# Slot attention into two mixture layers: phi held stationary for the P products, buffers named one by one, a new list of issue

## The chip, the cores and the metric

The kernel runs on one core of a Trainium2 chip. The metric is the device time of one execution in microseconds (us), the median of three runs. A profile of one execution goes with it. A difference of 0.3% (1.4 us) is about what a measurement of this kernel can tell from no change.

## The reference

Eight samples of eight heads are computed, 576 positions and head dimension 64, all in fp32:

```python
a = softmax(phi, axis=2)                      # 8 x 8 x 576 x 32, over the 576 positions
k_m, v_m = a^T k, a^T v                       # 32 memory rows per head
attn = softmax(q k_m^T / 8)                   # 576 x 32 per head
x = concat_heads(attn v_m)                    # 4608 x 512
h = max(x w1, x w2, x w3)                     # 4608 x 768
y = h w_out                                   # 4608 x 512, input of the second layer
logits = y phi2                               # 4608 x 32, 8 experts of 4 slots
slot_in = softmax(logits, axis=0)^T y
slot_out[e] = relu(slot_in[e] w1e[e]) w2e[e]  # 8 experts, 512 -> 1024 -> 512
out = softmax(logits, axis=1) slot_out
```

## The kernel before, in words

The 4608 x 512 matrix x is never formed. For a sample n the kernel multiplies its eight v_m by the weights first (V1 = v_m w, `v1m`, L563) and then the attention by V1 (`mn`, L596). The 768 columns of h are worked in six chunks i of 128. A unit is a pair (n, i): 48 units. For each unit there are two halves hf of 288 positions and three weights r, so 288 products `mn`, each of six matmuls (the attention and V1 are split into a high and a low part, `ah`, `al`, `vh`, `vl`) into one of three PSUM banks `m`. `ev` empties the bank: ACT copies r = 0 to g1 (L606), DVE takes the maximum for r = 1 (L608) and for r = 2 into ht (L610).

Stages of a sample, in the order in which they depend on each other: load phi transposed (`phit`), its maximum (`mxr`, DVE L373), exponential (`pe`, ACT L389), transpose on PE (`ptm`, L396) and copy (`ptc`, L401); k_m and v_m (`km`, 40 matmuls for the two halves of the heads, L438), normalized (`kmr`, `kmc`), transposed (`kvtm`, `kvtc`); scores (`scm`, L474), transposed by DVE (`sct`, L480), softmax (`s1r`, `s1s`, `s1e`, `s2s`, `s2m`), transposed back (`s3t`, L517), split into `ah` (ACT `s3h`, L527) and `al` (POOL `s3l`, L531). `vh` and `vl` are the split of V1 (`v1h` ACT L572, `v1l` DVE L578). For n = 0 the whole chain has to run before the first product can.

The weights come as 64-bit words and are brought to fp32 on the chip, in 17 chunks x: load (`raw`), ReLU with a scale on ACT (`cva`, L310) into a scratch buffer cz, a scaling of the low word on ACT (`cvb`, L314), a shift on DVE (`cvd`, L319), an addition on POOL (`cvp`, L324, 1.3 us for 512 columns and 1.8 for 768).

P = w_out phi2 (768 x 32) gives the logits straight from h. Before, each of its six chunks is a transpose of w_out (`pt`, L333), a copy (`pc`) and four matmuls with the transposed weights stationary and phi2 moving (`pm`, L342), and a copy (`po`).

`warm n` is n matmuls of the identity with itself (L800) that nothing reads. A matmul of fp32 has two records in the trace (a transpose one). In the tail, the eight experts are computed from 64 pieces of weights of 512 KB (`send`, one DMA each on SP's queue, L287; a few in four parts, L285). 44 buffers hold pieces; the first pieces are sent during the main part, into space of finished stages. The pieces of `more2` (L287, 383 us) need the space that the last `mn` and `ev` give up. Then come the remaining sends, as the experts give buffers up, and 18 output DMAs of 512 KB (L1091).

What sets the order of the work is a list written out by hand, `ORDER`: each word calls one of the functions above, every engine and SP's queue work in the order of this list, and semaphores do the rest. PSUM banks and the buffers g1, ht, vh and vl come from pools; which buffer a request gets is left to the pool.

Of the kernel before, what the change touches and what calls it, by code (L numbers as in the profile page):

```python
# [8 lines left out]
FR = mybir.dt.float32r  # L9
# [13 lines left out]
for _x in (2, 3, 4, 5, 12, 6, 7, 13, 8, 9, 14, 15, 10, 11):  # L23
# [135 lines left out]
)  # L159
W = [1, 0, 0, 3, 2]  # L160
NH = 4
LL = 0
# [1008 lines left out]
```

## Time and profile before

| | us |
|---|---|
| median of three runs (453.47 to 454.70) | 454.24 |
| the profiled execution, its own time | 454.55 |
| its span, first to last instruction | 452.8 |
| mean granted TensorE clock | 0.986 |

The span lies 1.75 us below the time of its own execution. Times in the rows are from the start of the span. In a chain of waits a row is: start, duration, engine, tile, line, records. In a timeline a row ends with what released the engine. A row with L800 is a warm product.

### The profile page before, as it was taken

To read this page: it belongs to the slowest core of one execution; us is meant where nothing else is said; L and a number is where in the kernel's file an instruction comes from. 1 tells how busy PE (TensorE), PEld (TensorE's weight loads), DVE (VectorE), ACT (ScalarE), POOL (GpSimd) and SP (SyncE) were. 2 spreads that over 40 slices of the span, in tenths; PEclk is the share of its full clock that TensorE was granted. 3 is DMA by queue.
4 is the path that set the end of the run, shared out by engine and by line. 5 is a ranking of instruction groups with operands and counts; after the bars stand their busy time and mean duration, and the time that the engine had idled before them with its cause. 6 is when DMAs were issued, how large, how long until landed. Compare 5 with 4: busy or idle time off the path is not lost.

```text
span 452.8 us, 12542 instructions
## 1 busy us (share of the span) xinstructions
PE 431.8 (95%) x5233; PEld 361.1 (80%) x5233; DVE 317.5 (70%) x736; ACT 192.3 (42%) x450; POOL 70.2 (16%) x92
## 2 busy tenths in 40 slices
PE   6989999999999999999999999999999999999990
PEld 5778889879888879978888887988887899655580
DVE  1275687578877996698779978898956453578480
ACT  2576777645443343343323342443434132222370
POOL 0243645520020003002100020020110000011000
PEclk9999999999999999999999999999999999999985
DMA  8987994307402293627657766378473956999997
GB/s 309 415 329 271 330 417 139 145 13 288 175 4 112 92 350 121 240 71 243 195 199 239 264 251 231 120 249 302 134 276 100 387 186 204 376 403 409 406 369 308
DMA packets 42249, 109.49 MB, mean 242 GB/s; under 512 B 3408, under 2 KB 20048, under 8 KB 40144
## 3 DMA queue, kind: packets, MB, share of 16 engines
q1 hardware_dynamic: 42192, 108.69, 65.5%
q8 instruction: 41, 0.67, 0.6%
q14 instruction: 16, 0.13, 0.1%
HBM read 91.38 MB, written 17.30 MB: 240 GB/s over the span
## 4 chain that ended last, share of the span: by engine, by line
PE 90%; DVE 3%; DMA 3%; ACT 1%; issue 1%; ACTq 0%; DVEq 0%
PE m L596 52%; PE x L563 8%; PE l L800 5%; PE x L438 4%; PE x L747 2%; PE l L679 2%; DMA more<-in_e_w_dram 2%; PE x L474 2%; PE m L1018 2%; PE x L638 2%; PE x L342 1%; PE l L1035 1%; PE x L1079 1%; PE m L1079 1%; PE x L333 1%
## 5 line engine op out<-in xcount | busy, mean ns | idle before, releaser
L596 PE MATMUL m<-ah,vh 128*128 128x288 f32 x576 | 171.0, 312 | 0.6 <-DVE ht L610 0.6
L596 PE MATMUL m<-ah,vl 128*128 128x288 f32 x576 | 161.6, 295 | 0.0
L596 PEld LDWEIGHTS m<-ah,vh 128*128 128x128 f32 x576 | 108.2, 188 | 19.3 <-issue 13.2
L596 PE MATMUL m<-al,vh 128*128 128x288 f32 x576 | 123.3, 295 | 0.0
L596 PEld LDWEIGHTS m<-ah,vl 128*128 128x128 f32 x576 | 108.4, 188 | 0.3
L596 PEld LDWEIGHTS m<-al,vh 128*128 128x128 f32 x576 | 92.3, 188 | 0.3 <-POOL al L531 0.3
L606 ACT ACTIVATE g<-m 128x288 f32<-128x288 f32 x96 | 39.1, 411 | 71.2 <-PE m L596 62.9
L608 DVE TENSOR_TENSOR g<-m,g 128x288 f32<-128x288 f32 x96 | 42.7, 450 | 33.8 <-PE m L596 28.4
L572 ACT ACTIVATE vh<-x 128x384 fp32r<-128x384 f32 (+1 forms) x100 | 42.0, 477 | 54.7 <-PE x L563 40.7
L610 DVE TENSOR_TENSOR ht<-m,g 128x288 f32<-128x288 f32 x96 | 42.5, 451 | 22.1 <-PE m L596 11.6
L578 DVE TENSOR_TENSOR vl<-x,vh 128x384 fp32r<-128x384 f32 (+1 forms) x100 | 48.8, 531 | 7.3 <-ACT vh L572 7.1
L563 PE MATMUL x<-arena,kvt 64*32 64x384 f32 (+1 forms) x800 | 39.5, 477 | 1.2 <-DVE vl L578 0.8
L531 POOL TENSOR_TENSOR al<-arena,ah 128x576 fp32r<-128x576 f32 x16 | 22.8, 1433 | 74.3 <-ACT ah L527 54.6
L800 PE MATMUL l<-cst 128*128 128x128 f32 x162 | 25.5, 307 | 4.0 <-DMA cst<-in_consts_dram 3.4
L324 POOL TENSOR_TENSOR arena<-arena 128x768 uint32<-128x768 uint32 (+1 forms) x13 | 23.5, 1811 | 34.8 <-ACT arena L314 27.4
L800 PEld LDWEIGHTS l<-cst 128*128 128x128 f32 x162 | 22.0, 211 | 7.3 <-DMA cst<-in_consts_dram 3.4
L615 POOL COPY arena<-ht 128x64 f32<-128x64 f32 x24 | 6.3, 279 | 123.7 <-DVE ht L610 97.8
L563 PEld LDWEIGHTS x<-arena,kvt 64*32 64x32 f32 x800 | 12.2, 105 | 13.6 <-issue 8.2
L642 DVE STREAM_TRANSPOSE arena<-ht 128x512 f32<-128x512 f32 x30 | 20.5, 697 | 0.2
L438 PE MATMUL x<-arena 128*32 128x129 f32 x640 | 19.6, 274 | 0.5 <-ACT arena L401 0.5
L438 PEld LDWEIGHTS x<-arena 128*32 128x32 f32 x640 | 17.4, 110 | 2.2 <-ACT arena L401 0.7
L480 DVE STREAM_TRANSPOSE arena<-x 128x288 f32<-128x288 f32 x32 | 13.4, 458 | 5.2 <-PE x L474 5.1
(266 smaller groups left out, 571.4 us busy)
## 6 DMA issues: line engine op xcount, KB each, us to landing
arena<-in_e_w_dram SPq DMA_DIRECT2D x44, 512.0 KB, 7.9
arena<-in_w_dram SPq DMA_DIRECT2D x14, 768.0 KB, 5.1
arena<-in_kv_dram SPq DMA_DIRECT2D x8, 1290.0 KB, 9.5
arena<-in_q_dram SPq DMA_DIRECT2D x16, 576.0 KB, 6.1
arena<-in_kv_dram SPq DMA_DIRECT2D x8, 1032.0 KB, 6.4
tr<-arena SPq DMA_DIRECT2D x30, 256.0 KB, 2.8
hbuf<-tr SPq DMA_DIRECT2D x30, 256.0 KB, 3.8
out_dram<-arena SPq DMA_DIRECT2D x10, 512.0 KB, 5.7
```

What stands on the lines that cost most here:

```text
L324: (eng or nc.gpsimd).tensor_tensor(out=du, in0=du, in1=lo.bitcast(U32), op=ALU.add)
L438: nc.tensor.matmul(t[32 * g:32 * g + 32, 0:KVC], phin_sb[:, j, b, 32 * g:32 * g + 32], kv_sb[:, j, b, g] if j < 4 else kv4_sb[:, g], start ...
L531: nc.gpsimd.tensor_tensor(out=al[n][:, :, c], in0=aT_sb[:, :, c], in1=ah[n][:, :, c].bitcast(FP32), op=ALU.subtract)
L563: nc.tensor.matmul(t[b][32 * g:32 * g + 32, 128 * r0:128 * r1], kvt[n][r, b, 32 * g:32 * g + 32], w_sb[r, i, r0:r1, g], start=True, stop=T ...
L572: nc.scalar.activation(out=v1[n, i][0][:, b, c], in_=ph["v1", n, i][b][:, c], func=ACTF.Copy)
L578: nc.vector.tensor_tensor(out=vl[:, b, c], in0=ph["v1", n, i][b][:, c], in1=vh[:, b, c].bitcast(FP32), op=ALU.subtract)
L596: nc.tensor.matmul(t[:, 0:HALF], x, y, start=(k == 0), stop=(k == 5))
L606: nc.scalar.activation(out=g1[u, hf], in_=t[:, 0:HALF], func=ACTF.Copy)
L608: nc.vector.tensor_tensor(out=g1[u, hf], in0=t[:, 0:HALF], in1=g1[u, hf], op=ALU.max)
L610: nc.vector.tensor_tensor(out=ht[n, i][:, cs], in0=t[:, 0:HALF], in1=g1.pop((u, hf)), op=ALU.max)
L642: nc.vector.transpose(out=v, in_=ht[n, i][:, 0:512])
L800: nc.tensor.matmul(t[:, 0:128], ident, ident, start=True, stop=True)
```

## The change

1. `ORDER` is replaced: the same work otherwise, in a new order on every engine and on SP's queue. `warm` is called for 34 products ahead of the steady part, where there were 81.
2. Banks and the buffers g1, ht, vh, vl are named one by one: a table `SLOTS` says for each request which buffer it takes.
3. The ReLU of the weights writes its destination, and the shift works on it in place; the four scratch buffers cz go.
4. P: phi2 is stationary in four column groups and three transposed chunks move at once (`pq`), a copy (`pr`), and three matmuls with that as the stationary operand and `sel` moving (`pm`), which add the four groups. Twice, for six chunks.
5. The first V (n = 0, i = 0), computed in three pieces r, has two banks of its own for each piece; before, the three pieces shared two banks.

```diff
-    "cst; warm 3; warm 2; warm 4; warm 3; warm 3; warm 1; phit 0; mxr 0; pe 0 0; pe 0 1; raw 2; warm 4; ptm 0 2; "
-    "ptm 0 0; warm 1; ptc 0 0; warm 4; ptm 0 1; ptc 0 1; warm 1; kv 0 0; km 0 1 0 2; kv 0 1; cva 2; cvd 2; raw 0; "
-    "ptc 0 2; cvb 2; cvp 2; cva 0; km 0 0 0 2; km 0 0 2 5; kmr 0 0; kmc 0 0; km 0 1 2 5; kmr 0 1; kmc 0 1; warm "
-    "3; kvtm 0; cvd 0; q 0 0; q 0 1; warm 1; kvtc 0; scm 0 0; sct 0 0; cvb 0; cvp 0; s1r 0 0; raw 1; cva 1; cvb "
-    "1; scm 0 1; sct 0 1; warm 1; warm 11; s1s 0 0; s1e 0 0; cvd 1; raw 3; cva 3; s1r 0 1; warm 4; raw 4; cvb 4; "
-    "cva 4; s2s 0 0; cvd 3; s2m 0 0; warm 9; cvp 1; s1s 0 1; v1m 0 0 1 2; v1h 0 0 1 2; v1m 0 0 0 1; cvb 3; v1h 0 "
-    "0 0 1; v1l 0 0 1 2; s3t 0 0; cvp 3; s1e 0 1; kv 1 0; phit 1; v1m 0 0 2 3; s3h 0 0; v1h 0 0 2 3; warm 8; warm "
-    "11; s2s 0 1; raw 6; cva 6; cvb 6; s3l 0 0; mn 0 0 1; mxr 1; pe 1 0; raw 5; warm 7; pe 1 1; cvd 4; ptm 1 0; "
...
-    "mn 47 1 2; mn 47 0 2; ev 47 1 1; trm 7 2; trc 7 2; ltm 0 3; dtm 6; dtc 6; ev 47 0 2; trm 7 1; trc 6 3; trc 6 "
-    "2; trm 7 4; trc 7 1; ev 47 1 2; trm 7 3; ltc 0 3; lg 7 1; slm 6 0; trc 7 3; slm 6 1; lg 7 2; lg 7 3; trc 7 "
-    "4; sla 6 0; sla 6 1; lg 7 4; hrc 47"
+    "phit 0; cst; warm 3; mxr 0; kv 0 0; pe 0 0; ptm 0 0; kv 0 1; warm 3; pe 0 1; ptm 0 1; ptm 0 2; ptc 0 2; raw "
+    "2; ptc 0 1; warm 3; km 0 1 0 2; warm 2; km 0 1 2 5; raw 0; ptc 0 0; km 0 0 0 2; cva 2; kmr 0 1; kmc 0 1; km "
+    "0 0 2 5; kmr 0 0; cvb 2; cvd 2; warm 3; cvp 2; kmc 0 0; kvtm 0; cva 0; cvd 0; q 0 0; kvtc 0; scm 0 0; warm "
+    "4; cvb 0; cvp 0; raw 1; cva 1; sct 0 0; q 0 1; warm 2; scm 0 1; s1r 0 0; cvb 1; s1s 0 0; cvd 1; cvp 1; warm "
+    "5; v1m 0 0 1 2; warm 2; sct 0 1; s1e 0 0; s2s 0 0; s2m 0 0; raw 3; cva 3; cvd 3; cvb 3; cvp 3; phit 1; v1h 0 "
+    "0 1 2; v1m 0 0 0 1; v1h 0 0 0 1; s3t 0 0; raw 4; s1r 0 1; warm 1; raw 5; v1l 0 0 0 1; s3h 0 0; s3l 0 0; cvb "
+    "4; warm 6; v1m 0 0 2 3; v1h 0 0 2 3; v1l 0 0 1 2; mn 0 0 1; cva 4; cva 5; mxr 1; pe 1 1; pe 1 0; v1l 0 0 2 "
+    "3; mn 0 0 2; s1s 0 1; s1e 0 1; cvd 4; kv 1 0; mn 0 0 0; ptm 1 2; ptc 1 2; ptm 1 1; ptc 1 1; cvd 5; ptm 1 0; "
+    "ptc 1 0; kv 1 1; ev 0 0 0; cvp 4; v1m 0 1; v1h 0 1; s2s 0 1; s2m 0 1; s3t 0 1; v1l 0 1; s3h 0 1; s3l 0 1; ev "
+    "0 0 1; km 1 1; km 1 0; cvb 5; cvp 5; raw 6; kmr 1 0; cvb 6; mn 1 0 0; ev 1 0 0; cva 6; ev 0 0 2; raw 7; kmc "
...
+    "44 1 2; ev 44 1 2; trc 6 4; mn 46 1 0; mn 46 0 0; ev 46 0 0; mn 44 0 2; ev 44 0 2; trm 7 1; trc 7 1; trm 7 "
+    "0; trc 6 3; dtm 6; dtc 6; trc 7 0; mn 46 0 1; ev 46 0 1; hrc 44; mn 46 1 1; ev 46 1 0; ev 46 1 1; mn 47 1 2; "
+    "slm 6 0; lg 7 0; lg 7 1; mn 47 0 1; mn 47 0 0; ev 47 1 2; hrc 47; ev 47 0 0; mn 47 0 2; mn 46 1 2; ev 47 0 "
+    "1; ev 47 0 2; mn 46 0 2; hrc 42; ltm 0 3; ev 46 1 2; trm 7 2; send 1; send 1; send 1; send 1; send 1; send "
+    "1; send 1; sla 6 0; trm 7 3; trc 7 3; ev 46 0 2; trm 7 4; trc 7 4; send 1; send 1; lg 7 2; lg 7 3; slm 6 1; "
+    "lg 7 4; sla 6 1; trc 7 2; hrc 45; send 1; send 1; send 1; ltc 0 3; hrc 46"
...
+    def buf(pool, tag, shape, dtype, count):
+        if tag not in picks:
+            return pool.tile(shape, dtype, tag=tag, name=tag, bufs=count)
+        j = int(next(picks[tag]))
+        if (tag, j) not in fixed:
+            fixed[tag, j] = pool.tile(shape, dtype, tag=tag + "_%d" % j, name=tag + "_%d" % j, bufs=1)
+        return fixed[tag, j]
+
     def bank(pool, tag):
-        return pool.tile([128, 512], FP32, tag=tag, name=tag)
+        return buf(pool, tag, [128, 512], FP32, {"m": 3, "x": 4, "l": 1}[tag])
...
-        nc.scalar.activation(out=z, in_=hi, func=ACTF.Prelu, scale=2.0 ** -112, alpha=2.0 ** 32)
+        nc.scalar.activation(out=dst, in_=hi, func=ACTF.Prelu, scale=2.0 ** -112, alpha=2.0 ** 32)
...
-        nc.vector.tensor_scalar(out=du, in0=zu, scalar1=3, scalar2=None, op0=ALU.logical_shift_left)
+        nc.vector.tensor_scalar(out=du, in0=du, scalar1=3, scalar2=None, op0=ALU.logical_shift_left)
...
-        for k in range(4):
-            nc.tensor.matmul(
-                t[:, 0:32], wt_sb[i][:, 128 * k:128 * k + 128], phi2_sb[:, k], start=(k == 0), stop=(k == 3))
+    def p_q(y):
+        ph["pq", y] = t = mx()
+        o = wt_all[y].rearrange("p (j k c) -> p k j c", j=3, k=4)
         for k in range(4):
             nc.tensor.matmul(
+                t[32 * k:32 * k + 32, 0:384], phi2_sb[:, k], o[:, k], start=True, stop=True, tile_position=(0, 32 * k))
+    def p_r(y):
+        nc.scalar.activation(out=pq_sb[y], in_=ph["pq", y][:, 0:384], func=ACTF.Copy)
+    def p_m(y):
+        ph["pm", y] = t = mx()
+        for j in range(3):
+            nc.tensor.matmul(
+                t[:, 32 * j:32 * j + 32], pq_sb[y][:, 128 * j:128 * j + 128], sel[:, 0:M], start=True, stop=True)
...
-        if ("v1", n, i) not in ph:
-            ph["v1", n, i] = [mx() for _ in range(2)]
-        t = ph["v1", n, i]
+        ph["v1", n, i, r0] = t = [mx() for _ in range(2)]
```

Both lists send 31 pieces before the tail. In the old one sends 18 to 29 stand together after 253 of the 288 products `mn`, 30 and 31 after 264 and 273. In the new one send 18 stands after 269, 19 after 273 and 20 to 31 after all 288; on SP's queue the last instruction ahead of these twelve is `trc 6 3`, which stands after 280; it waits for turns (`trm 6`, a transpose on DVE and a DMA) of which the last stands after 264.

## Rows read from the trace of the kernel before

**Rows 1.** The page: busy time by engine, and the chain's shares by engine.

```profile
PE 431.8 (95%) x5233; PEld 361.1 (80%) x5233; DVE 317.5 (70%) x736; ACT 192.3 (42%) x450; POOL 70.2 (16%) x92
PE 90%; DVE 3%; DMA 3%; ACT 1%; issue 1%; ACTq 0%; DVEq 0%
```

**Rows 2.** Stretches: PE, PEld, DVE, ACT, POOL busy us (instructions), granted clock, DMA share, GB/s.

```profile
0.00:10.00 10.00, 6.47 (x24) 5.42 (x24) 1.61 (x4) 2.72 (x3) 0.60 (x6) 1.00 0.82 294
10.00:20.00 10.00, 9.20 (x129) 7.82 (x128) 1.66 (x6) 4.51 (x11) 1.30 (x1) 1.00 1.01 416
...
60.00:70.00 10.00, 10.00 (x100) 9.10 (x85) 7.78 (x17) 7.02 (x14) 3.94 (x3) 1.00 0.91 367
```

**Rows 3.** The chain of waits, 0 to 60 us: start, us, what ended last.

```profile
6.35 2.09 PE l L800 x8
...
11.62 1.16 PE l L800 x8
...
16.00 2.41 PE x L438 x80
...
20.15 1.21 PE x L474 x32
...
35.75 0.80 PE m L596 x6
...
43.97 0.73 PE m L596 x4
```

**Rows 4.** Timelines of DVE, ACT, POOL and PE, 0 to 50 us.

```profile
5.02 1.35 DVE L373 TENSOR_REDUCE pmax<-arena 128x2 f32<-128x1152 f32 x1 [4.12 <-DMA arena<-in_phi_t_dram]
...
20.95 0.85 DVE L480 STREAM_TRANSPOSE arena<-x 128x288 f32<-128x288 f32 x2 [1.54 <-PE x L474]
...
30.40 0.83 DVE L517 STREAM_TRANSPOSE arena<-arena 128x288 f32<-128x288 f32 x2
...
6.61 1.44 ACT L389 ACTIVATE arena<-arena,pmax 128x576 f32<-128x576 f32 x2 [0.26 <-DVE pmax L375]
...
29.87 1.84 POOL L324 TENSOR_TENSOR arena<-arena 128x768 uint32<-128x768 uint32 x1 [4.12 <-ACT arena L314]
...
32.02 1.44 POOL L531 TENSOR_TENSOR al<-arena,ah 128x576 fp32r<-128x576 f32 x1 [0.30 <-ACT ah L527]
...
30.34 0.64 PE L563 MATMUL x<-arena,kvt 64*32 64x128 f32 x16 [0.83 <-DVE vl L578]
```

**Rows 5.** The chain of waits again: P products, a like product, and products after others.

```profile
47.90 0.80 PE m L596 x6
...
62.17 0.81 PE x L342 x8
...
93.09 0.99 PE m L596 x6
...
198.88 1.29 PE x L747 x16
```

**Rows 6.** The page's groups: matmuls of the products, and DVE's emptying of the second.

```profile
L596 PE MATMUL m<-ah,vh 128*128 128x288 f32 x576 | 171.0, 312 | 0.6 <-DVE ht L610 0.6
...
L608 DVE TENSOR_TENSOR g<-m,g 128x288 f32<-128x288 f32 x96 | 42.7, 450 | 33.8 <-PE m L596 28.4
```

**Rows 7.** SP's timeline near the end, and stretches there.

```profile
346.59 0.81 SPq L287 DMA_DIRECT2D more<-in_e_w_dram  x2
...
373.21 1.60 SPq L287 DMA_DIRECT2D arena<-in_e_w_dram  x2
...
383.02 2.24 SPq L287 DMA_DIRECT2D more<-in_e_w_dram  x5
...
380.00:384.00 4.00, 4.00 (x83) 3.01 (x84) 1.87 (x4) 2.66 (x6) 0.24 (x1) 1.00 0.03 6
...
404.00:412.00 8.00, 7.54 (x140) 4.17 (x136) 7.57 (x21) 3.13 (x7) 2.30 (x2) 1.00 1.03 411
...
448.00:450.00 2.00, 0.00 (x0) 0.00 (x0) 0.00 (x0) 0.00 (x0) 0.00 (x0) 0.50 0.96 381
```

More of the change, by code (lines that the diff above doesn't have):

```diff
@@ L29 @@
 ORDER = (
[129 rows of a table removed]
-)
[128 rows of a table added]
+)
+SLOTS = {
+    "g1": (
+        "012021210120120201201201210210120210210212012012021201202212201202012102120112110202120120100120"
+    ),
+    "ht": (
+        "012301210132103201320132032102301230210320130231"
+    ),
+    "m": (
+        "0122021010210120102102120120102200101010210220121212120200201210212002020121210210211021012020202101"
+        "1120102102022120121201012021020202020102120210212102120120210202010112020212012012021010120210210210"
+        "2021020120120120120121020201210210202120201201021120101012012202010102020120120101021012012021010101"
+        "0102102102102102102102"
+    ),
+    "vh": (
+        "012021201021021201202102102102102120120102102101"
+    ),
+    "vl": (
+        "012021201021021201202102102102102120120102102101"
+    ),
+    "x": (
+        "0123210321032121032103210231310231023102323213030212301230123012301302130213032103210321321020231230"
+        "1230123012130213023231203120312031201320132021302103210321032103131023102323102323102310231023231023"
+        "1023231032013201320132013201302121203231012301230123012301230123012301230123012301230123"
+    ),
+}
 W = [1, 0, 0, 3, 2]
@@ L200 @@
     gp = main_x.enter_context(tc.tile_pool(name="gp", bufs=3))
+    picks = {k: iter(v) for k, v in SLOTS.items()}
+    fixed = {}
+    def buf(pool, tag, shape, dtype, count):
[5 more added lines that the diff above has]
+        return fixed[tag, j]
     def bank(pool, tag):
-        return pool.tile([128, 512], FP32, tag=tag, name=tag)
+        return buf(pool, tag, [128, 512], FP32, {"m": 3, "x": 4, "l": 1}[tag])
     def mx():
@@ L243 @@
     x0 = a0 + 12288
-    lt2 = lt_all.rearrange("p r c -> p (r c)")
-    cz = [h5x[:, 0:768], h5x[:, 768:1536], s_run, lt2[:, 0:768]]
-    wt_ht = hbuf[:, 0]
-    wt_sb = [wt_ht[:, 512 * j:512 * j + 512] for j in range(3)]
-    wt_sb += [arena[:, x0 + 512 * j:x0 + 512 * j + 512] for j in range(3)]
+    wt_all = [hbuf[:, 0], arena[:, x0:x0 + 1536]]
+    wt_sb = [w[:, 512 * j:512 * j + 512] for w in wt_all for j in range(3)]
+    pq_sb = [h5x[:, 384 * y:384 * y + 384] for y in range(2)]
     hr = [arena[:, o:o + 768].rearrange("p (i c) -> p i c", i=NI) for o in (x0 + 4608, x0 + 5376)]
@@ L305, in cv_view @@
         dst = arena[:, c:c + w] if c < 9216 else wo_sb[:, c - 9216:c - 9216 + w]
-        return v[:, :, 0], v[:, :, 1], cz[x % 4][:, 0:w], dst
+        return v[:, :, 0], v[:, :, 1], dst
     def cv_a(x):
-        lo, hi, z, dst = cv_view(x)
-        nc.scalar.activation(out=z, in_=hi, func=ACTF.Prelu, scale=2.0 ** -112, alpha=2.0 ** 32)
+        lo, hi, dst = cv_view(x)
+        nc.scalar.activation(out=dst, in_=hi, func=ACTF.Prelu, scale=2.0 ** -112, alpha=2.0 ** 32)
     def cv_b(x):
@@ L316, in cv_d @@
     def cv_d(x):
-        lo, hi, z, dst = cv_view(x)
-        zu, du = z.bitcast(U32), dst.bitcast(U32)
-        nc.vector.tensor_scalar(out=du, in0=zu, scalar1=3, scalar2=None, op0=ALU.logical_shift_left)
+        lo, hi, dst = cv_view(x)
+        du = dst.bitcast(U32)
+        nc.vector.tensor_scalar(out=du, in0=du, scalar1=3, scalar2=None, op0=ALU.logical_shift_left)
     def cv_p(x, eng=None):
-        lo, hi, z, dst = cv_view(x)
+        lo, hi, dst = cv_view(x)
         du = dst.bitcast(U32)
@@ L337, in p_c, with p_o @@
         nc.scalar.activation(out=wt_sb[i], in_=ph["pt", i], func=ACTF.Copy)
-    def p_m(i):
-        ph["pm", i] = t = mx()
+    def p_q(y):
+        ph["pq", y] = t = mx()
+        o = wt_all[y].rearrange("p (j k c) -> p k j c", j=3, k=4)
         for k in range(4):
             nc.tensor.matmul(
-                t[:, 0:32], wt_sb[i][:, 128 * k:128 * k + 128], phi2_sb[:, k], start=(k == 0), stop=(k == 3))
-    def p_o(i):
-        nc.scalar.activation(out=p_sb[:, i], in_=ph["pm", i][:, 0:32], func=ACTF.Copy)
+                t[32 * k:32 * k + 32, 0:384], phi2_sb[:, k], o[:, k], start=True, stop=True, tile_position=(0, 32 * k))
[6 more added lines that the diff above has]
+                t[:, 32 * j:32 * j + 32], pq_sb[y][:, 128 * j:128 * j + 128], sel[:, 0:M], start=True, stop=True)
+    def p_o(y):
+        nc.scalar.activation(
+            out=p_sb[:, 3 * y:3 * y + 3].rearrange("p i m -> p (i m)"), in_=ph["pm", y][:, 0:96], func=ACTF.Copy)
     kvt, ah, al = {}, {}, {}
@@ L568, in v1_h @@
         if (n, i) not in v1:
-            v1[n, i] = [vp.tile([128, 2, 384], FR, tag=x, name=x) for x in ("vh", "vl")]
+            v1[n, i] = [buf(vp, x, [128, 2, 384], FR, VP) for x in ("vh", "vl")]
         c = slice(128 * r0, 128 * r1)
         for b in range(2):
-            nc.scalar.activation(out=v1[n, i][0][:, b, c], in_=ph["v1", n, i][b][:, c], func=ACTF.Copy)
+            nc.scalar.activation(out=v1[n, i][0][:, b, c], in_=ph["v1", n, i, r0][b][:, c], func=ACTF.Copy)
     def v1_l(n, i, r0=0, r1=3):
@@ L578, in v1_l @@
             nc.vector.tensor_tensor(
-                out=vl[:, b, c], in0=ph["v1", n, i][b][:, c], in1=vh[:, b, c].bitcast(FP32), op=ALU.subtract)
+                out=vl[:, b, c], in0=ph["v1", n, i, r0][b][:, c], in1=vh[:, b, c].bitcast(FP32), op=ALU.subtract)
     ht = {}
@@ L603, in ev @@
             if (n, i) not in ht:
-                ht[n, i] = ring.tile([128, S], FP32, tag="ht", name="ht", bufs=4)
-            g1[u, hf] = gp.tile([128, HALF], FP32, tag="g1", name="g1")
+                ht[n, i] = buf(ring, "ht", [128, S], FP32, 4)
+            g1[u, hf] = buf(gp, "g1", [128, HALF], FP32, 3)
             nc.scalar.activation(out=g1[u, hf], in_=t[:, 0:HALF], func=ACTF.Copy)
@@ L825 @@
             msr=lambda: nc.gpsimd.memset(s_run, 0.0),
-            cva=cv_a, cvd=cv_d, cvb=cv_b, cvp=cv_p, cvq=cv_q, pt=p_t, pc=p_c, pm=p_m, po=p_o,
+            cva=cv_a, cvd=cv_d, cvb=cv_b, cvp=cv_p, cvq=cv_q, pt=p_t, pc=p_c, pq=p_q, pr=p_r, pm=p_m, po=p_o,
             mxr=mx_r, mxd=mx_d, pe=pe_e, ptm=pt_m, ptc=pt_c, bcm=bc_m, bcs=bc_s, bce=bc_e, km=km_m, kmr=km_r, kmc=km_c, kvtm=kvt_m, kvtc=kvt_c,
```

230 rows, old and new, of the table ORDER are left out of this document.

## The prediction

> **What bounds the kernel now.** Read the page first: PE is busy for 95% of the span and holds 90% of the chain that ended last, so time is gained only where PE waits, does work nobody needs, or works less [rows 1]. Then the stretches: PE has gaps in the first 20 us and none at 60 to 70 us, where it is busy 10.00 of 10 us; DMA runs at 294 and then 416 GB/s [rows 2]. So the start is a separate problem from the middle. The chain of the start shows which: attention's chain for sample 0 is waited for, and what stands in its place on PE are warm products (L800). One group of eight records takes 2.09 us at 6.35 and 1.16 us at 11.62 [rows 3], 0.26 and 0.145 us a record: half speed first (1.2 against 2.4 GHz), though the granted column of that stretch shows 1.00 [rows 2]. The first product ends at 36.55 (35.75 and 0.80), but steady work begins only at 43.97, after three products, ten transposes, the next V1 and the `km` of sample 1 [rows 3]. In both lists the same work precedes that point; only the order and the warm products differ. Last, the tail: DMA is idle at 380 to 384 us (share 0.03) and from then on nearly full (1.03 at 404 to 412, still 0.96 at 448 to 450) [rows 7]. So the end is bound by bytes that may be sent only from 383.02 on, when the last product's space is free: 31 pieces and 18 outputs of 0.524 MB, 25.7 MB at about 0.4 MB/us, some 65 us of the 69.8 left. An earlier end of the main part is passed on, unless DMA enters the tail with a backlog.
>
> **The start, worked out by legs.** I follow the new list with the durations of before.
> (a) To the end of `km`. Phi is first on SP's queue now, ahead of the 0.2 MB of constants; its maximum begins at about 4.4 instead of 5.02, and after 1.35 and 1.44 us [rows 4] both exponentials are done at about 7.5. PE may start when the constants land, at about 5.0 (before, phi, second in the queue, had landed then). It has three groups of three warm products (18 records) and ten transposes in front of `km`, 28 records at 0.26 us: 12.3. `km` takes 2.41 [rows 3] and the two warm products within it 0.5: 15.2, against 18.41. k and v pass raw 2 on the queue: 3.17 MB ahead of the end of k and v, at 294 GB/s to 10 us and 416 after [rows 2], are in by about 11.5. Not late.
> (b) To the scores: 20.15 less 18.41 is 1.74 before [rows 3]; ACT now has weight passes between, I allow 2.05: 17.25.
> (c) To the softmax, transposed back. Before: 30.40 and 0.83, so 31.23 [rows 4], 11.1 after the scores. There DVE's list has V1's subtraction (`v1l 0 0 1 2`) ahead of `s3t`, and DVE waited for V1 on PE and for its split on ACT. In the new list that subtraction stands behind `s3t`, and the second half's passes mostly too: between the scores' landing (0.8 after their start, 20.95 less 20.15) and the end of `s3t` are eight passes of 0.5 to 1.2 us, the transposes of 0.85 and 0.83 the first and last [rows 4]; I count 6.6 us. 17.25 + 0.8 + 6.6 = 24.65.
> (d) To `al`: before 33.46 (32.02 and 1.44) [rows 4], 2.2 after `s3t`. Now a weight addition of 1.84 [rows 4] is ahead on POOL and costs 0.3 more: 27.15.
> (e) To the first product: 35.75 before, 2.3 later, because nineteen warm products are in front. The new list has none there: 27.2.
> (f) To steady work: 8.2 before, with seven warm products (14 records at 0.145, 2.0). Without these 6.2; I add 1.6, since the second product now waits for a subtraction that DVE's list puts behind the next sample's maximum (1.35 [rows 4]): 7.8, **35.0**.
> Gain 9.0 us. Bounds: 10.5, if nothing waits but what I counted; 5, if the V1 pieces still queue behind ACT as before. The first V's own banks are in this: before, PE stood 0.83 us for the subtraction of one piece [rows 4]. In-place ReLU changes no instruction's size; I price it at nothing, since the shift depends on the ReLU anyway; the waits of `cva` for an old scratch buffer go. Cover gone, it costs a DVE pass of about half a us. Late next, after 35 us, is ACT: three weight passes stand ahead of `v1h 0 2`. Products of two units cover them.
>
> **P.** Before: six `pm` of 0.81 [rows 5], 4.86 us on PE. After: two `pq`, four matmuls of 384 columns in column groups; that shape is the slot product L747, two of which take 1.29 [rows 5], so 0.65 each. Two `pm` of three matmuls, six records at the 0.1 of a 128x32 record: 0.61 each. Sum 2.5. A product after column-tiled work takes 0.99, after a 128x128 transpose 0.80 [rows 5]; twice that 0.19 for `pq` is 0.4. Gain **2.0** (1.5 to 2.4). ACT does four copies in place of six, off the path. The row of 1.29 already holds one entry into column-tiled work, so I add nothing for entries. A rule speaks against that: by the Trainium skill, TensorEngine Tiling, Key Properties, every change of the tiling mode drains the engine, the entry too. If each entry cost another 0.19, P would gain 1.6, and the time would be 444.9.
>
> **Order in the middle.** Counted in the lists, products follow other work 64 times instead of 70 after the point of 43.97. At 0.19 after column-tiled work and nothing after the rest [rows 5], taken half and half, that is **0.5** us gained.
>
> **Named banks.** `SLOTS` gives 67 of the 288 products the bank of the product before last, with one product of 0.80 as the time to empty it. Emptying on DVE takes 0.45, and a matmul's record of 0.31 [rows 6] goes on some 0.18 after the next matmul starts (0.80 for six is 0.13 each), so it just fits if DVE starts at once. It waited for PE 28.4 us over 96 times [rows 6], so it is often, not always, ready. 27 of the 67 are DVE's; 20 late by 0.1 are **2.0 us lost**. Bounds 0 and 0.25 for each of the 67, 17.
>
> **The end.** The space for the `more2` pieces was free at 383.02 [rows 7], when the last maxima were done, and these stood behind turns of sample 7. In the new list three of those turns and `ltm` (15 transposes, at 0.1 as for L342's records, 1.5 us) stand behind the last product, while one slot product (0.65) has moved ahead of it: the space is free **0.9** earlier in the order of PE's work. Against it, on SP's queue: before, pieces 19 and 20 left at 346.59 with ten more behind, and the last two at 373.21; DMA was idle by 380 [rows 7]. New: twelve pieces stand behind `trc 6 3`, and it waits only for turns after product 264; some 22 products of 0.80, 18 us, and 2 us of other work are left then. Two pieces go just ahead and two more behind: sixteen of 1.28 us (0.524 MB at 411 GB/s [rows 7]) are 20.5 us, so DMA enters the tail with a little left: **0.7 lost** (0 to 3).
>
> **Sum** against the profiled execution's 454.55: -9.0 - 2.0 - 0.5 + 2.0 - 0.9 + 0.7 = -9.7, 444.85. The median is 0.31 lower: **444.5**.
>
> **Rivals.**
> R1, slower: banks. The reuse after one product decides. It has its place in all of the middle; the price is the lateness times 67. At 0.18 us each, 12 us, it eats the gain of 9.7 and the 2.0 counted already; at 0.25 it costs 16.8 in place of 2.0, and the time is 459. For it: DVE is 70% busy [rows 1] and 78% at 60 to 70 us [rows 2]. Against: 40 of the 67 are ACT's, at 42%.
> R2, the tail swallows it: pieces sent later are bytes left over. If trc 6 3 is held up by 5 us, five us of DMA go over: 449.5. For it: DMA has no slack from there on [rows 7]. Against: `trc 6 3` needs little of the other engines.
> R3, the clock. 47 warm products fewer. Warm records are at half speed at 6.35 and at full at 11.62, after warm products without a break [rows 3]. If half speed lasts through scores and the first V, roughly 6 us of PE work are done twice: 450.5. Against: the new list leaves gaps of well under 1 us in my legs. The Trainium skill, TensorE: Matmul & The Clock Gate, Part 1, has half rate as the default which activity releases; the trace agrees, the first group is the slow one.
> R4, no change: naming buffers cannot win in the middle, since PE is full there [rows 2], and the start's gain is lost to DVE and ACT, which must do the same passes: 454.
>
> **How the numbers follow.** Forecast 0.66, R1 0.10 (slower), R2 0.10, R3 0.09, R4 0.05. Faster by over 0.3%: 0.85; within 0.3% (about what a measurement of this kernel can tell): 0.05; slower: 0.10. The forecast's own range is 439.5 (all bounds on the good side: 1.5 of the start, 2 of the banks, 0.7 of the tail, and 0.7 of the rest) to 448.5 (the start gains 5). Taking in R2 and R3 it is 439.5 to 451; R1, R4 are left out, and some of the forecast's edges.
>
> **What would show it.** Right: `km` of sample 0 ends near 15, the first product starts near 27, steady work from 35; the four `pq` matmuls overlap, 0.65 a group; `more2` is sent about 10 us earlier and DMA has no gap there; then some 70 us to the end. Wrong: PE idle before L596 released by L606, L608 or L610 summing to over 5 us (R1); more than 71 us after the `more2` sends (R2); warm or `km` records at half speed past 14 us (R3); steady work later than 39 us.

## The result, and the profile after

The changed kernel took 446.32 us (median of 4 runs, 446.26 to 447.3) beside 454.21 (453.47 to 454.7) for the kernel before on the same chip: ratio 0.983, 95% interval 0.981 to 0.985. That is 7.9 us less, where 9.7 were forecast (444.5 us, range 439.5 to 451). The profiled execution has a span of 444.5 us, 8.3 less than the span of before; what follows is reckoned in these two spans.

The page of the changed kernel, parts 1 and 4 (busy time by engine; shares of the chain):

```profile
PE 419.1 (94%) x5119; PEld 344.9 (78%) x5119; DVE 312.9 (70%) x736; ACT 192.4 (43%) x448; POOL 69.7 (16%) x92
PE 85%; DMA 5%; DVE 4%; ACT 1%; issue 1%; POOL 0%; SPq 0%; ACTq 0%; DVEq 0%
```

Beside [rows 1], PE is busy 12.7 us less and DVE's work is unchanged within 5 us; PE's share of the chain fell from 90 to 85%, so more of the chain lies outside PE. The chain of waits at the start shows where (start, us, what ended last); it answers to [rows 3]:

```profile
0.74 4.08 DMA arena<-in_phi_t_dram
...
13.45 1.94 PE x L482 x64
...
17.28 0.82 PE x L518 x16
...
23.21 10.45 DMA arena<-in_kv_dram
...
33.71 1.97 PE x L482 x64
35.67 4.99 PE m L638 x36
```

The `km` of sample 0 ends at 15.39 (13.45 and 1.94), the scores start at 17.28, and steady work (products without a break: L638 in one run of 36, right after the `km` of sample 1) begins at 35.67, against 43.97 [rows 3]: 8.3 us earlier. The last thing ahead of it is new: K and V of sample 1 land at 33.66. PE's list of waits puts that at 0.8 us, and shows the two largest waits of the middle:

```profile
PE x L721 <- DVE ht L652: 1.1, 1, 1.1
...
PE x L482 <- DMA arena<-in_kv_dram: 0.8, 1, 0.8
...
PE x L789 <- DMA hbuf<-tr: 0.8, 1, 0.8
```

The middle, from the start of steady work to the last sample's maximum on DVE, holds the same instructions on PE but for P (570 products of each kind in both). That maximum is L855 before and L897 after:

```profile
L855 DVE TENSOR_REDUCE hbuf<-l x1: 324/324/324, 384.6 to 384.6; 128x1 f32<-128x160 f32 x1
```

```profile
L897 DVE TENSOR_REDUCE hbuf<-l x1: 325/325/325, 376.9 to 376.9; 128x1 f32<-128x160 f32 x1
```

The sums of busy time over that stretch (PE's first; after "mean" the same per row), 43.97 to 384.6 before and 35.67 to 376.9 after:

```profile
sum 340.63, PE 339.75 PEld 294.47 DVE 259.81 ACT 147.88 POOL 55.88; mean PE 48.54 PEld 42.07 DVE 37.12 ACT 21.13 POOL 7.98
```

```profile
sum 341.23, PE 339.35 PEld 290.44 DVE 255.23 ACT 149.09 POOL 54.85; mean PE 42.42 PEld 36.30 DVE 31.90 ACT 18.64 POOL 6.86
```

So the middle did not get shorter: 341.2 us against 340.6, with 1.88 us idle on PE against 0.88. From the last maximum to the end it is 67.6 us against 68.2. The whole difference is 8.3 at the start, 0.6 back in the middle, 0.6 gained at the end.

### The profile page after: what moved, and what is told of

Its sections match the earlier page's. It is cut to its first block, busy times and chain, and to the rows that moved or that the text cites. A ratio compares the mean times of both kernels' runs of the same rounds, so it can differ in the third digit from the quotient of the medians.

```text
span 444.5 us, 12325 instructions
## 1 busy us (share of the span) xinstructions
PE 419.1 (94%) x5119; PEld 344.9 (78%) x5119; DVE 312.9 (70%) x736; ACT 192.4 (43%) x448; POOL 69.7 (16%) x92
## 4 chain that ended last, share of the span: by engine, by line
PE 85%; DMA 5%; DVE 4%; ACT 1%; issue 1%; POOL 0%; SPq 0%; ACTq 0%; DVEq 0%
PE m L638 51%; PE x L605 7%; PE x L482 4%; PE x L789 3%; DMA arena<-in_kv_dram 2%; PE l L721 2%; PE m L1060 2%; DMA hbuf<-tr 2%; PE x L518 2%; PE m L1077 2%; PE x L680 2%; PE x L1121 1%; PE l L1077 1%; DMA arena<-in_phi_t_dram 1%; PE m L1121 1%
## 5 line engine op out<-in xcount | busy, mean ns | idle before, releaser
L638 PE MATMUL m<-ah,vh 128*128 128x288 f32 x576 | 170.2, 310 | 0.0
L638 PE MATMUL m<-ah,vl 128*128 128x288 f32 x576 | 162.0, 296 | 0.0
L638 PEld LDWEIGHTS m<-ah,vh 128*128 128x128 f32 x576 | 108.1, 188 | 21.3 <-issue 11.7
L638 PE MATMUL m<-al,vh 128*128 128x288 f32 x576 | 123.4, 295 | 0.4 <-POOL al L575 0.4
L638 PEld LDWEIGHTS m<-ah,vl 128*128 128x128 f32 x576 | 108.3, 188 | 0.6 <-DVE vl L620 0.3
L638 PEld LDWEIGHTS m<-al,vh 128*128 128x128 f32 x576 | 92.3, 188 | 0.8 <-POOL al L575 0.8
L650 DVE TENSOR_TENSOR g<-m,g 128x288 f32<-128x288 f32 x96 | 42.6, 447 | 30.1 <-PE m L638 15.2
L357 POOL TENSOR_TENSOR arena<-arena 128x768 uint32<-128x768 uint32 (+1 forms) x13 | 22.9, 1769 | 28.0 <-ACT km L493 15.2
L605 PEld LDWEIGHTS x<-arena,kvt 64*32 64x32 f32 x800 | 11.3, 105 | 12.2 <-issue 8.3
L842 PE MATMUL l<-cst 128*128 128x128 f32 x68 | 11.7, 315 | 5.5 <-DMA cst<-in_consts_dram 5.3
L842 PEld LDWEIGHTS l<-cst 128*128 128x128 f32 x68 | 9.8, 217 | 7.6 <-DMA cst<-in_consts_dram 5.3
```

What stands on the lines that cost most here:

```text
L357: (eng or nc.gpsimd).tensor_tensor(out=du, in0=du, in1=lo.bitcast(U32), op=ALU.add)
L605: nc.tensor.matmul(t[b][32 * g:32 * g + 32, 128 * r0:128 * r1], kvt[n][r, b, 32 * g:32 * g + 32], w_sb[r, i, r0:r1, g], start=True, stop=T ...
L638: nc.tensor.matmul(t[:, 0:HALF], x, y, start=(k == 0), stop=(k == 5))
L650: nc.vector.tensor_tensor(out=g1[u, hf], in0=t[:, 0:HALF], in1=g1[u, hf], op=ALU.max)
L842: nc.tensor.matmul(t[:, 0:128], ident, ident, start=True, stop=True)
```

## Experiments

Each kernel was timed beside the kernel before, whose median was 454.16 for the first four experiments, 453.82 for the next four and 454.21 for the last three. The ratios are to these. The first four ask which part of the change carries the gain.

**The new start on the old kernel.** The new list up to the `km` of sample 1, then the old list's remaining operations.

```diff
 ORDER = (
-    <the old list>
+    <the new list, to "km 1 1; km 1 0">; <the old list without these operations and without warm>
```

> The kernel before, with the operations of the new list up to the keys' product of sample 1 put first and all its other operations after them in their old order; old products for P, scratch buffers, pools. Theory (the start is nearly the whole gain): steady work begins near 35.7 us instead of 43.97 and the rest runs as before, so 8 us less (7 to 9), 446 us. Rival 1 (the new start only borrows from the weights' conversion, which then runs late in the old list): 2 to 5 us less. Rival 2 (the gain comes from P, the buffers and the rest of the list): under 2 us less.

Measured: 451.96 us, ratio 0.995 (0.993 to 0.997), 2.2 us less. The chain shows why so little:

```profile
31.87 8.11 DMA arena<-in_w_dram
...
40.05 0.88 ACT arena L315
40.93 0.30 ACT g L607
...
41.28 1.06 PE m L597 x6
```

PE's timeline over the same time has:

```profile
32.80 2.41 PE L439 MATMUL x<-arena 128*32 128x129 f32 x80
...
41.28 0.40 PE L597 MATMUL m<-ah,vh 128*128 128x288 f32 x1 [3.03 <-ACT g L607]
```

The start itself came: the `km` of sample 1 (L439) ends at 35.2, where before it ended at 43.97. The seam then cost part of it. Three products follow, and PE stands for 3.03 us. In the old list the conversion of weight piece 8 (L315) is ahead of the emptying of a product (L607), and ScalarE works in order. The piece was sent at 31.87, when POOL's addition had freed its place, and took 8.11 us to land. ScalarE itself stood idle for only 1.05 us of these; the 8 us of waiting in the expectation of the longer start below is the transfer's time. Of the lead of 8.8 us, 5.3 are left behind the seam (the next transposes of weights at 51.12, against 56.45) and 4.7 in the span (448.1). The profiled execution was the fastest of six (449.84; the others 451.86 to 452.68), so what the median lost more stands in no trace. By size and cause this is rival 1. It decides nothing yet about the rest.

**No warm products at the start.** All 34 of the list are left out (the expectation counts 35).

```diff
-    "phit 0; cst; warm 3; mxr 0; kv 0 0; pe 0 0; ptm 0 0; kv 0 1; warm 3; pe 0 1; ...
+    "phit 0; cst; mxr 0; kv 0 0; pe 0 0; ptm 0 0; kv 0 1; pe 0 1; ...
```

> The changed kernel with the warm products of the list (35 in the start) left out; they compute nothing that is used. Theory (the start is set by the chain of loads, sums and copies, and the clock counts only for the products between): first products of sample 0 at half speed, steady work some 3 us later (1.5 to 6), 449 us. Rival 1 (the clock is the whole gain of the start): 8 us or more back, 454 us or above. Rival 2 (PE waits so much in the start that speed is free): within 1 us of the changed kernel.

Measured: 447.05 us, ratio 0.985 (0.983 to 0.986), within the interval of the changed kernel. This is rival 2; the theory's 3 us did not come. First two stretches of the changed kernel, then the same of this one (the column before the last two is the granted clock):

```profile
10.00:20.00 10.00, 8.71 (x139) 6.72 (x145) 3.90 (x10) 6.24 (x13) 2.60 (x2) 1.00 1.01 412
20.00:36.00 16.00, 13.63 (x219) 10.17 (x204) 13.88 (x34) 13.44 (x26) 8.50 (x6) 1.00 0.98 388
```

```profile
10.00:20.00 10.00, 6.54 (x114) 4.22 (x114) 4.13 (x10) 5.97 (x12) 2.58 (x2) 0.90 1.01 411
20.00:36.00 16.00, 11.69 (x175) 9.76 (x176) 13.76 (x35) 13.06 (x26) 7.74 (x5) 0.64 0.97 390
```

and its chain:

```profile
10.94 4.22 PE x L483 x80
...
35.59 1.01 PE m L639 x6
```

The clock does drop (0.64 at 20 to 36 us), and the 80 matmuls of `km` take 4.22 us. But they start 1.2 us earlier, at 10.94 instead of 12.16, as no warm products stand ahead, and end at 15.16 where the changed kernel's end at 15.39. Steady work begins at 35.59, as early as with them, though not quite without a break: PE is busy 23.72 of the 24 us from 36 to 60, where the changed kernel fills 24.00. The clock is not what the start gained.

**P by the old form**, in the changed kernel's list.

```diff
-    "... pq 0; pr 0; mn 3 1 2; trc 0 0; pm 0; phin 2; po 0; ...
+    "... pm 0; po 0; mn 3 1 2; trc 0 0; pm 1; pm 2; phin 2; po 1; po 2; ...
-    "... pq 1; pr 1; ... pm 1; po 1; ...
+    "... pm 3; po 3; ... pm 4; pm 5; po 4; po 5; ...
```

> The changed kernel with P by the old form: six groups of four products of 32 columns with the weights stationary and six small evictions, at the places of the new ones. Theory (the term of the sum): 2.0 us slower (1.5 to 2.4), as TensorE is busy on both sides of each. Rival 1 (a product's cost goes by its columns alone): 1.6 us slower or less. Rival 2 (hidden): within 0.5 us.

Measured: 449.74 us, ratio 0.992 (0.989 to 0.995), 3.4 us slower than the changed kernel, though its six runs lie far apart (448.58 to 453.27); in the profiled executions the span is 447.0, 2.5 more. The theory's sign, at the upper end of its size or above. The pieces of P in the chain of waits, in the kernel before (beside the one of 0.81 at 62.17 [rows 5]) and in the changed one:

```profile
72.10 1.70 PE x L342 x16
...
90.24 0.81 PE x L342 x8
...
112.89 0.81 PE x L342 x8
...
123.38 0.81 PE x L342 x8
```

```profile
65.79 0.78 PE x L376 x8
...
67.56 0.59 PE x L385 x6
...
98.77 0.65 PE x L376 x8
...
102.51 0.60 PE x L385 x6
```

4.94 us became 2.62: 2.3 less. By the busy time of the groups it is 2.5 (5.7 and 3.2), but there each group also holds the time in which it overlaps its neighbours.

**Buffers from the pools instead of by name.**

```diff
-SLOTS = {"g1": ..., "ht": ..., "m": ..., "vh": ..., "vl": ..., "x": ...}
+SLOTS = {}
```

> The changed kernel with its list, but every rotating buffer taken from its pool in turn instead of by name. Theory after the trace (no product waited long for a named bank): within 1.5 us of the changed kernel. Rival 1 (the prediction's term: the named banks stand closer together and cost 2 us): about 2 us faster. Rival 2 (the list needs the names, since a pool hands out a bank that is not yet read): 3 us slower or more.

Measured: 445.09 us, ratio 0.980 (0.979 to 0.982), 1.2 us less than the changed kernel; the two intervals overlap a little. So the list works without the names, and the theory holds. The traces differ most at one place, 100 to 110 us, first the changed kernel, then this one:

```profile
100.00:110.00 10.00, 8.91 (x126) 6.89 (x117) 6.56 (x17) 3.90 (x10) 0.41 (x2) 1.00 0.82 282
```

```profile
100.00:110.00 10.00, 10.00 (x123) 8.28 (x120) 7.05 (x18) 3.90 (x10) 0.41 (x2) 1.00 0.88 303
```

The 1.09 us that PE is idle there are its wait for DVE at the logits of sample 1 (L721), in the list above. All three kernels with named buffers have it (1.1 here, 1.1 without warm products, 0.9 with the old P); none of the seven kernels that run this part of the new list with pools has it. Which of the named buffers makes it stays open.

The next four turn the question of the start round, and try a version that beats both.

**A longer new start on the old kernel**, so that the seam lies behind the crowded conversion of the weights.

```diff
-    <the new list, to "km 1 1; km 1 0">; <the old list without these operations and without warm>
+    <the new list, to "v1l 1 0; cvb 10">; <the old list without these operations and without warm>
```

> As start_alone, but the new list is kept further, through the scores of sample 1 and the conversion of weight piece 10, so that no piece of the weights is converted at the seam; then the old list's remaining operations in their order. Theory (start_alone lost its start at the seam, where ScalarE waited 8 us for a weight piece ahead of the evictions): steady work at 35.7 us and some 8 us less than before, 446 to 447 us. Rival (a start ahead of the weights is paid back later, whatever the seam): 2 to 4 us less, 450 to 452 us.

Measured: 448.80 us, ratio 0.988 (0.985 to 0.990), 5.0 us less than before: between the two. Steady work does begin early, but two stretches of the middle lose time:

```profile
35.44 1.01 PE m L596 x6
...
40.55 5.95 DMA arena<-in_w_dram
```

```profile
48.00:52.00 4.00, 3.57 (x45) 2.83 (x38) 3.90 (x11) 3.58 (x7) 1.87 (x1) 1.00 1.02 404
56.00:60.00 4.00, 2.79 (x21) 2.56 (x20) 3.64 (x5) 1.75 (x4) 3.69 (x3) 1.00 1.00 417
```

PE is idle 0.43 and 1.21 us there while DVE is busy 3.90 and 3.64 of 4 us and DMA is full: an early start meets the conversion of the weights, which did not come earlier with it. The old order of the rest gives part of the gain back: 1.64 us in these two places; the span is 6.3 us less than before.

**The old start on the changed kernel** (with pools).

```diff
-    <the new list>
+    <the old list, to "scm 1 1; sct 1 1 ... s1e 1 0", with its warm products>; <the new list's rest>
```

> The changed kernel with pools, its first operations (through the first exponentials' ends of sample 1) in the old list's order with its warm products, the rest in the new order. Theory (the start is worth 8 us and is not made up later): steady work at 44 us, some 8 us slower than the changed kernel with pools at 445.1, 453 us. Rival (the rest of the new list, P and buffers carry the gain): 447 us or less.

Measured: 453.62 us, ratio 0.999 (0.997 to 1.001): 8.5 us slower than with the new start (445.09). The `km` of sample 1 (L460 on PE's timeline) ends at 42.39, against 35.65 with pools and the new start:

```profile
39.98 2.41 PE L460 MATMUL x<-arena 128*32 128x129 f32 x80
```

So 6.7 of the 9.3 us between the two spans (452.4 and 443.1) are lost at the start. This seam has a price too: PE is idle 0.90 us at 50 to 70 us, where it has no gap with pools, and the middle is 2.0 us longer in all. With the old start, everything else that was changed is worth nothing that can be measured, P included.

**Three moves in the list**, at the three places where the trace after shows time.

```diff
-    raw 4; ... raw 5; ... kv 1 0; ... kv 1 1; ...
+    raw 4; ... kv 1 0; kv 1 1; raw 5; ...
-    trm 2 5; trm 3 0; ... trm 3 1; ... kv 5 1; ... kv 5 0; ... trc 2 3; ... trc 2 5;
+    trm 2 5; trc 2 3; trm 3 0; ... trm 3 1; trc 2 5; ... kv 5 1; ... kv 5 0; ...
-    late; mn 43 0 2; rtm 1 2; rtc 1 2; ... rsm 1; ... <sends 18 to 29>
+    late; mn 43 0 2; rtm 1 2; rtc 1 2; send 1 (x4); ... rsm 1; send 1 (x8); ...
```

> The changed kernel with pools and three moves in its list: both loads of sample 1's K and V ahead of weight piece 5; the two transposed halves of sample 2 (pieces 3 and 5) ahead of the loads of sample 5; sends 17 to 28 of the experts' weights as soon as their places are free. Theory: 0.85 from the keys' wait at 33.7, 0.8 from the wait at 199, 0.85 from the transfers' backlog into the tail, 2.5 us together, 442.6 us. Rival (what is saved in front is waited for at the next stage, and the experts' weights set the end): within 1 us of 445.1.

Measured: 457.57 us, ratio 1.007 (1.005 to 1.010), 12.5 us slower than with pools alone: a miss, and the most telling run of all. (The sends moved are 18 to 29 of the list's 31; the expectation counts them from 0.) Two of the three moves broke something. The start, in the chain:

```profile
22.41 10.99 DMA arena<-in_w_dram
...
34.21 1.43 ACT arena L410 x2
...
35.69 2.35 PE x L417 x10
```

Weight piece 5 was issued no earlier than 22.4 and now shares the queue with K and V; it lands at 33.40. Its conversion on ACT stands ahead of sample 1's exponentials (L410), so the transposes (L417) come at 35.69 and steady work at 41.61. And near the end:

```profile
348.19 8.71 DMA tr<-arena
...
356.99 0.71 DVE arena L661
357.70 0.91 DVE vl L597 x2
358.60 0.38 DVE g L627
...
359.02 3.01 PE m L615 x11
```

A turn through memory was issued behind seven pieces sent from 340.41 on, four of them moved there, and took 8.71 us to land. DVE's next transpose needs its buffer (L661), DVE stands in order, the emptying of a product (L627) is behind, and PE is idle for 6.0 us. The stall has a second price: behind it PE runs for some 4 us at a granted clock of 0.50 (1.2 GHz), and a product takes 1.44 us in place of 0.80. Two stretches, the clock in the column before the last two:

```profile
359.00:361.00 2.00, 1.98 (x8) 1.98 (x9) 1.08 (x2) 0.13 (x1) 0.00 (x0) 0.50 0.19 66
...
365.00:367.00 2.00, 2.00 (x17) 2.00 (x16) 0.63 (x3) 0.41 (x1) 0.00 (x0) 1.00 0.90 317
```

Of the 12.8 us by which the last maximum comes later (388.2, against 375.4 with pools), 5.96 are the start and 6.0 the stall; the wait of 0.95 that the halves' move saves is gone; what is left, 1.8, is by difference, and the slow clock accounts for about as much.

The early sends did relieve DMA (0.80 at 375 to 385 us, where the kernel with pools has 1.04 in the ten us before its `more2` sends), and the time from the last maximum to the end was 67.9 us, against 67.7 with pools. So the transfers carried into the tail had cost nothing that shows.

**The ReLU in scratch again** (with pools).

```diff
-        nc.scalar.activation(out=dst, in_=hi, func=ACTF.Prelu, scale=2.0 ** -112, alpha=2.0 ** 32)
+        nc.scalar.activation(out=z, in_=hi, func=ACTF.Prelu, scale=2.0 ** -112, alpha=2.0 ** 32)
-        nc.vector.tensor_scalar(out=du, in0=du, scalar1=3, scalar2=None, op0=ALU.logical_shift_left)
+        nc.vector.tensor_scalar(out=du, in0=zu, scalar1=3, scalar2=None, op0=ALU.logical_shift_left)
```

> The changed kernel with pools and the ReLU of the weights written to the four scratch buffers of before instead of in place (and the clearing of the running sum after the last conversion that uses it as scratch). Theory: the same instructions on the same engines, nothing waits for the scratch, within 0.5 us of 445.1. Rival (a fourth piece waits for the scratch of the first in the crowded start): 1 to 3 us slower.

The clearing of the running sum, which is one of the scratch buffers, moves behind the last conversion that uses it. Measured: 445.95 us, ratio 0.981 (0.978 to 0.984): not told apart from pools. In place is worth under what can be measured here, though not for want of waits: the trace has 1.5 us of PE waiting for ACT's emptying (L627) that pools does not have, and not pools' wait of 0.7 for the keys.

The last three take two of the moves apart and test the loads.

**The halves alone** (with pools): `trc 2 3` and `trc 2 5` moved as above, nothing else.

> The changed kernel with pools and only one of the three moves of pools_three: the transposed halves of sample 2 (pieces 3 and 5) ahead of the loads of sample 5. Theory (in pools_three this wait went, 40.00 of 40 us busy between 180 and 220 where pools has 39.05, and the loss came from the other two): 0.9 us less than pools, 444.2 us. Rival (the loads of sample 5 now come late): 445.1 us or more.

Measured: 444.22 us, ratio 0.978 (0.976 to 0.981). PE's stretch with pools, then here:

```profile
180.00:220.00 40.00, 39.05 (x425) 32.60 (x424) 30.54 (x69) 14.93 (x37) 4.09 (x8) 1.00 0.49 168
```

```profile
180.00:220.00 40.00, 40.00 (x432) 33.41 (x430) 31.31 (x71) 15.64 (x38) 4.11 (x8) 1.00 0.47 169
```

The wait of 0.95 is gone, and the median is 0.9 less, as the theory had it. The two intervals overlap, so it is the trace that shows it.

**Keys first, with the conversion out of the way** (the halves' move kept). The loads of sample 1 ahead of piece 5 as above, and `cva 5`, `cvd 5` moved behind `km 1 0`.

> As halves_first, with the loads of sample 1's K and V ahead of weight piece 5 again, and the conversion of that piece on ScalarE and VectorE moved behind the keys' product of sample 1, so that the exponentials of sample 1 no longer stand behind it on ScalarE. Theory (in pools_three ScalarE waited for piece 5 until 33.4 us and the exponentials and transposes of sample 1 came 5.2 us late): that wait goes and the keys' 0.85 too, 0.85 less than halves_first. Rival (piece 5 and what follows it in the load queue are now late for the first products of V): 1 us or more above halves_first.

Measured: 443.43 us, ratio 0.976 (0.974 to 0.979). The loss of the three moves is gone, but the gain is not shown: the profiled spans are 442.4 here and 442.3 for the halves alone, and the intervals overlap. The keys are no longer waited for: on PE's timeline the `km` of sample 1 (L459) runs

```profile
32.02 2.41 PE L459 MATMUL x<-arena 128*32 128x129 f32 x80
```

and ends at 34.4, where it ends at 35.5 for the halves alone. Two products later the chain names the next in line, the conversion on ACT and DVE:

```profile
34.65 1.08 DVE arena L329
...
36.41 3.63 PE m L615 x24
```

At 102 us a lead of 0.7 us is left, at the last maximum 0.1. PE's list of waits has 0.2 us in between; where the rest went is open.

**The old order of the first loads** (with pools).

```diff
-    "phit 0; cst; ... kv 0 0; ... kv 0 1; ... raw 2; ... raw 1; ... q 0 1; ...
+    "cst; phit 0; ... raw 2; kv 0 0; ... kv 0 1; ... q 0 1; raw 1; ...
```

> The changed kernel with pools, only the order of the first loads as before: constants ahead of phi, weight piece 2 ahead of K and V, the second half of Q ahead of weight piece 1. Theory (the first part of the start is the loads' turn: 512 KB more stand ahead of K and V at some 390 GB/s): steady work 1.3 us later, 446.4 us. Rival 1 (compute and not loads sets the start): within 0.5 us of 445.1. Rival 2 (the order of the loads is most of the start's gain): 449 us or more.

Measured: 445.73 us, ratio 0.981 (0.979 to 0.984), 0.6 us above pools and nearest to rival 1. Steady work begins at 35.84 instead of 35.65 with pools. The turn of the first loads is worth 0.2 us of the start; the rest of it is, by elimination, the order of the work on PE, DVE and ACT, with the later loads and the first V's banks in it.

## Why the prediction was right, step by step

| term | forecast | shown |
| --- | --- | --- |
| start | -9.0 | -8.3 by the trace; 8.5 back when undone (in the spans 9.3, 6.7 of it at the start) |
| P | -2.0 | -2.3 by the chain; 3.4 back when undone, 2.5 by the spans |
| order in the middle | -0.5 | +1.9, by difference |
| named banks | +2.0 | +1.1, one wait; 1.2 back when undone |
| end and backlog | -0.2 | -0.6 |

**The start** was right in mechanism and close in its legs: `km` ended at 15.39 (forecast 15.2), the scores began at 17.28 (17.25), the first product at 26.22 (27.2), steady work at 35.67 (35.0). The leg that fell short is the last, 9.45 us where 7.8 were forecast: "Late next, after 35 us, is ACT". It was DMA first, 0.8 us, since on SP's queue the keys of sample 1 stand behind weight piece 5, which waits for its place to be free; this queue was not followed past the first loads.

**P** was right, a little too small. The further loss at each entry into column-tiled work, which would have left 1.6, does not show: chain and run are both above 2.0.

**Order in the middle** has the wrong sign. PE's busy time there fell by 0.4 us though P saves 2.3, so the same other matmuls take 1.9 more; counting how often products follow other work did not foresee it, and no run here says which change of kind costs it. Two waits came in addition, one for the transposed halves of sample 2 (0.8) and the one of the names; 0.88 us of waits of before went. Together that is the 0.6 by which the middle is longer: -2.3, +1.9 and 1.88 less 0.88.

**Named banks**: a price of about 1 us, but not by the mechanism of the sum. The 67 close reuses cost no wait that the list of PE's waits shows; the price is a single wait at the logits. That this term and the end came out better than forecast, by 0.9 and 0.4, made up for about half of the 2.4 by which the order came out worse: that the total lies within 2 us of the forecast is partly luck.

**The end.** `more2` is free 9.2 us earlier (373.85, against 383.02 [rows 7]); about 10 were forecast:

```profile
373.85 2.23 SPq L320 DMA_DIRECT2D more<-in_e_w_dram  x5
```

From there it is 70.65 us to the end where before had 69.8, which looked like the forecast backlog of 0.7. It is not: measured from the last maximum the tail is no longer, in the kernel with the early sends either. The pieces merely leave earlier than PE's work ends: 3.05 us ahead of the last maximum, against 1.58 before.

**The rivals.** R1 (banks) falls with the waits: nothing near 5 us. R2 (the tail) falls with 67.6 against 68.2 us. R3 (the clock) falls twice: on PE's timeline of the changed kernel six records of warm products take 1.65 us at 5.34, 1.49 at 8.17 and 0.83 at 10.72, so the full rate is there by then, and without any the time is the same. R4 said the start's gain would be lost to DVE and ACT; it does not happen with the new rest of the list, but with the old rest the gain was 5.0 and not 8.5 us, and part of what was lost (1.64 us) was lost just so. The gain belongs to the start and to a rest that fits it, and the forecast spoke only of the first.

Not tried: the first V's own banks and the later loads, each apart from the rest of the start.

## What to carry over

In a kernel that one engine fills, a gain at the start is kept only if the next stage's work can begin earlier too; try it from both sides, the new start on the old rest and the old start on the new rest. Before moving a transfer forward, list what stands behind it: on its queue, on the engine that consumes it in order, and behind the buffers it shares with short round trips; two of three such moves here cost 6.0 and some 7.8 us, and each was meant to save 0.85. The best version found is the new list with pools, the halves ahead of the loads, and perhaps the keys first: 443.43 to 444.22 us.

## What was not expected of the hardware

Warm products bought nothing: without them the granted clock was 0.64 at 20 to 36 us, the level of 1.2 GHz for most of that stretch, after PE had been busy 6.54 of the 10 us before, and the median was 0.7 us higher, with intervals that overlap. The Trainium skill, TensorE: Matmul & The Clock Gate, Part 1, has the full rate as something that sustained activity earns; the trace agrees with that (0.64 without the warm products, 1.00 with them), but here the slower matmuls filled waits for loads and for other engines: even at the lower clock PE was busy only 11.69 of the 16 us.

The first transfer of a turn, 256 KB, lands in 2.3 us (median of the 30 of the kernel with pools; the longest took 6.3); behind seven pieces of 512 KB issued just before it on the same queue one took 8.71 us.
